# A DeltaNet block with a Fourier-mixing MLP on one core: the first sequence's opening is put in another order, and its first MLP products run ahead

## The chip, the cores and the metric

The kernel runs on 1 core of a Trainium2 chip. The core has TensorE (PE, matrix products into PSUM), VectorE (DVE), ScalarE (ACT), GpSimd (POOL) and SyncE (SP, whose queue issues most DMA transfers). Each of them works through its own instructions in a fixed order. The metric is the device time of one execution in microseconds.

## The reference

Inputs are q, k, v of shape (4, 8, 768, 48) in float32, beta of shape (4, 8, 768), and two weight matrices in float64. First a delta rule, for each of 4 sequences and 8 heads, with a 48 x 48 state:

```
k_n = k / (norm(k) + 1e-6)
for t in range(768):
    y[t]  = q[t] @ state
    v_old = k_n[t] @ state
    state = state + beta[t] * outer(k_n[t], v[t] - v_old)
```

The heads are laid side by side, which gives x of shape (4, 768, 384). Then:

```
mixed = real(fft(fft(x, axis=seq), axis=model))
u  = x + mixed
un = (u - mean(u)) / sqrt(var(u) + 1e-6)
out = u + max(un @ w_ch1, 0) @ w_ch2          # 384 -> 1536 -> 384
```

All is computed in float32 on the chip.

## The kernel before

**Delta rule.** A "load" g is 128 positions of one sequence, all 8 heads; a sequence has 6 loads (NL), 24 in all. A load is two chunks of 64 positions. Within a chunk the sequential rule becomes the inverse of a triangular matrix of 64 x 64. `pre_a` (L297) transposes the keys to KT on PE and forms their products G and GU. `invert16` (L432) inverts, for four loads at a time (a "round"), the 16 x 16 diagonal blocks by 15 pairs of DVE instructions (L491, L494), and then transposes the result on DVE to G and A (L497, L499). `pre_m16` (L572), for the loads 0 to 11, builds the whole inverse from these: Z and MT are masked copies on ACT (L582, L594), followed by four products on PE (Z with GU, MT with ND, Z with ND, MT with ND), with DVE steps at L605 and L609 and ACT steps at L591 and L607 between them; V is scaled at L613; for the loads 0 to 5 it then forms WT and U (L634, L635) in 32 small products of MT with K and V. `pre_q` (L505) makes QT and the masked product LQ (L529). `step(g, c)` (L641) is the recurrence, two dependent PE-DVE hops per chunk, and `outputs` (L705) gives x in two parts (L725 on ACT, L735 on DVE).

**Fourier part.** `folds` (L742) forms sums and differences of x along the sequence and the model axis, 8 DVE instructions for each of three t. `fourier` (L777) multiplies them with the tables evt and odt on PE (`sums`, into PSUM tiles pf), copies the result to F on ACT (L814), mirrors F (L819), and for each of six blocks T of 128 positions multiplies F with dtab and adds to x on DVE (L837 to L845), with mean and variance; POOL makes rstd (L848, L849).

**MLP.** `mlp` (L853): a group g is two blocks T. `scaled` makes un (L863), transposes it on PE (ptr) to unT (L868). Then 12 first products ph for fc = 0 to 11, each with Relu to hT (L880), and for each of the two blocks a second product po of 12 parts, added to x and stored (L890, L891). With its yields the MLP of one sequence has 75 pieces.

**Weights.** `weights` (L221) loads float64 as pairs of 32-bit words in twelve pieces of 768 KB, six of w1 (256 columns, i.e. two fc, each) and six of w2, two in flight, and converts each one: ACT L257, DVE L259, L261, L263, ACT L266, DVE L268, L269, POOL L272. A piece has five yields; `convert(n)` takes n of them for w1, w2's six follow in `conv`.

**Order.** Up to the end of the first products of sequence 0 the order of PE, DVE, ACT and POOL is written out by hand: generators are advanced one yield at a time (`advance`, `drain`, `fill` for inverse 1 and the folds). A loop over g = 0 to 5 does the recurrence of load g beside `pre_m16` of loads g+1 and g+2, the conversion of w1 and, from g = 4, the folds and keys of round 2. After it come the Fourier part and the first MLP products. From there on only PE's order is written out; the other engines' order is set by a scheduler. `period(g)` (L942) does the loads 6 to 23, six slots each, and advances the MLP of the sequence before (`side`) to a given number of pieces per slot (L1000); for sequence 0 thirteen pieces are done when it starts. `conv` and inverse 2 (for the loads 8 to 11) run under the first of these periods.

**Buffers.** A tag names a set of buffers that tiles share in turn: "big" has two (LQ6, the weights' ring, hT), "unT" two, "F" one, "M" one, "O" one; PSUM has the tags "pair", "one" and "post", two buffers each.

Of the kernel before, what the change touches and what calls it, by code (L numbers as in the profile page):

```python
# [20 lines left out]
RL = 4  # L21
# [43 lines left out]
def kernel(  # L65
# [15 lines left out]
    NC = NL  # L81
# [139 lines left out]
    def weights():  # L221
# [21 lines left out]
        for i, (_, dst) in enumerate(pieces):  # L243
            if i % half == 0:
                ring = wk.tile([128, 2, n, 2], I32, tag="big", bufs=2, name="w64")
                stage(i)
                stage(i + 1)
                yield
            lo, hi = ring[:, i % 2, :, 0], ring[:, i % 2, :, 1]
            if i < half:  # L250
                man = wk.tile([128, n], F32, tag="unT", bufs=2, name="man")
                num = wk.tile([128, n], I32, tag="unT", bufs=2, name="num")
            else:
                tmp = wk.tile([128, 2, n], F32, tag="O", name="wtmp")
                man, num = tmp[:, 0], tmp[:, 1].bitcast(I32)

            nc.scalar.activation(man, lo.bitcast(U32), ACT.Copy, scale=2.0 ** -52, bias=1.0)  # L257
            yield
            nc.vector.tensor_scalar(num, hi, 0xFFFFF, None, op0=ALU.bitwise_and)  # L259
            yield  # L260
            nc.vector.scalar_tensor_tensor(man, num, 2.0 ** -20, man, op0=ALU.mult, op1=ALU.add)  # L261

            nc.vector.tensor_scalar(num, hi, 20, 0x7FF, op0=ALU.logical_shift_right,  # L263
                                    op1=ALU.bitwise_and)
            yield
            nc.scalar.activation(num, num, ACT.Relu, bias=low_e)  # L266
            yield
            nc.vector.tensor_scalar(num, num, 255, 2.0 ** 23, op0=ALU.min, op1=ALU.mult)  # L268
            nc.vector.scalar_tensor_tensor(num, hi, -2 ** 31, num, op0=ALU.bitwise_and,  # L269
                                           op1=ALU.bitwise_or)  # L270
            c = dst.shape[1]
            nc.gpsimd.tensor_tensor(dst, man.rearrange("p (c f) -> p c f", c=c),  # L272
                                    num.bitcast(F32).rearrange("p (c f) -> p c f", c=c),
                                    op=ALU.mult)
            if i % half + 2 < half:
                stage(i + 2)
            yield
# [294 lines left out]
    def pre_m16(g):  # L572
# [20 lines left out]
        for e in range(2):  # L593
            nc.scalar.activation(MT[:, :, e, :], MTd[:, m8, :], ACT.Copy, scale=m_blk[:, e:e + 1])  # L594
        flat = "p m b t -> p (m b t)"
        yield
        for i in range(3):
# [14 lines left out]
        V = Vs.pop(g)  # L612
        (nc.vector if g < 2 * RL else nc.gpsimd).tensor_tensor(  # L613
            V.rearrange("p c j d -> p (c j) d"), V.rearrange("p c j d -> p (c j) d"),
            nT[:, m8, None].broadcast_to([128, 8, D]), op=ALU.mult)
# [161 lines left out]
    def fourier(b):  # L777
# [8 lines left out]
        def sums(a, par, tab, n, ts):  # L786
            if ts[0] == 0:
                pas[a, par] = ps_one()[:, 0:2 * n].rearrange("p (i k) -> p i k", i=2) if b else \
                    ps_post([128, 2, n], "pf")
# [9 lines left out]
        for a in range(2):  # L799
            for par, tab, n, hi in tabs:  # L800
                if b or a:
                    sums(a, par, tab, n, range(TH))
                elif par == 0:
                    for p2, t2, n2, _ in tabs:
                        sums(0, p2, t2, n2, range(TH - 1))
                    yield
                    for p2, t2, n2, _ in tabs:
                        sums(0, p2, t2, n2, (TH - 1,))
# [8 lines left out]
            for i in range(2 * a, 2 * a + 2):  # L817
                n = parts[i][2] - parts[i][1]
                nc.scalar.activation(F[0:n, i, HALF + 1:SEQ], F[0:n, i, HALF - 1:0:-1], ACT.Copy)  # L819

        norms = normed[b] = []
        for T in range(NC):
            tt = T % GT
            ks = slice(128 * T, 128 * T + 128)

# [27 lines left out]
    def mlp(b):  # L853
# [17 lines left out]
        unT = scaled(0)  # L871
        yield
        for g in range(NC // GT):
            hT = wk.tile([128, KF, GT * 128], F32, tag="big", bufs=2, name="hT")
            for fc in range(KF):
                ph = ps_post([128, GT * 128], "ph")
                for dt in range(KD):
                    mm(ph, w1[:, dt, 128 * fc:128 * fc + 128], unT[:, dt, :], dt == 0,
# [3 lines left out]
            for tt in range(GT):  # L882
                T = GT * g + tt
                po = ps_post([128, DM], "po")
                for fc in range(KF):
                    mm(po, hT[:, fc, 128 * tt:128 * tt + 128], w2[:, fc, :], fc == 0,
                       fc == KF - 1)
                    if fc % 2 == 1 and fc < KF - 1:
                        yield
                nc.vector.tensor_tensor(x[:, T, :], x[:, T, :], po, op=ALU.add)  # L890
                nc.sync.dma_start(out=out_v[b, T], in_=x[:, T, :])  # L891
                yield

                if tt == 0 and g + 1 < NC // GT:
                    unT = scaled(g + 1)
                    yield

# [44 lines left out]
    def period(g, side):  # L942
# [43 lines left out]
        for i in range(SLOTS):  # L986
# [13 lines left out]
            want = (PIECES - KEEP) * (SLOTS * n + i + 1) // (SLOTS * NL)  # L1000
# [8 lines left out]
    with tc.manual_schedule(engines=engines):  # L1009
# [48 lines left out]
        spin(1)  # L1058
        drain(qs[0])
        advance(ms[0])  # L1060
        advance(ms[1], 2)
# [3 lines left out]
        advance(qs[1])  # L1065
        drain(keys[-1])
        advance(ms[0])
        advance(ms[1])
        advance(inv1, 6)
        drain(ms[0])  # L1070
        advance(ms[1])
# [3 lines left out]
        fd = iter(())  # L1075
# [15 lines left out]
        for g in range(NL):  # L1091
# [4 lines left out]
            if g > 0:  # L1096
                advance(c0)
                fill(3)
            if g > 1:
                convert(1)  # L1100
            if g == 2:
                drain(inv1)
            if g > 0:
                advance(nm)
                advance(late)
            advance(n2)
            advance(c0)
            fill(3)
            if g == 0:
                advance(nm)  # L1110
            advance(n2)
            if g > 0:
                drain(late)
            if g == 4:
                fold = folds(0)
            if g >= 4:
                fd = part(fold, 8)
                advance(keys[g - 4])
            if g + 1 < NL:
                drain(qs[g + 1])  # L1120
            advance(nm)
            advance(c1)
            fill(3)
            if g > 0:
                convert(2)
            drain(nm)
            advance(n2)
            if g + 1 < NL:
                advance(c1)
            fill(3)  # L1130
            if g > 0:
                convert(2)
            advance(n2)
            if g + 2 < NL:
                advance(qs[g + 2])
            if g >= 4:
                drain(keys[g - 4])
# [5 lines left out]
            if g == 2:  # L1143
# [3 lines left out]
                load_q(NL + 1)  # L1147
        convert(1)
        drain(late)
        late = None  # L1150
        drain(ms[-1])
        load_beta(2)

        drain(fold)
        f = fourier(0)
        advance(f)
        for i in range(4):
            advance(f)
            convert((2, 1, 1, 1)[i])
        advance(keys[2])  # L1160
        advance(f)
        drain(keys[2])
        advance(f)
        advance(keys[3])
        side, done = mlp(0), 0
        advance(side)
        drain(keys[3])
        for T in range(2, NC):
            while converted < min(30, 5 * (T // 2 + T % 2)):
                convert(1)  # L1170
            advance(f)
            advance(side)
        for fc in range(NC - 2, KF):
            while converted < min(30, 5 * (fc // 2 + 1)):
                convert(1)
            advance(side)
        done = 1 + KF
# [48 lines left out]
```

## Time and profile before

| | us |
|---|---|
| median of 3 runs | 797.94 |
| the runs | 794.44, 797.94, 798.23 |
| profiled execution | 796.16 |
| its span | 794.4 |

| engine | busy us | share of the span |
|---|---|---|
| PE | 704.1 | 89% |
| PE weight loads | 544.2 | 69% |
| DVE | 372.5 | 47% |
| ACT | 243.9 | 31% |
| POOL | 99.2 | 12% |

Between span and time lie 1.8 us outside the first and last instruction. The 40 slices of the span (19.9 us each; digits are busy tenths, and tenths of full clock for PEclk) show where PE is not busy:

```profile
PE   5876676777599989999989999699999999999998
DVE  5857657569841496425189117984121141600000
ACT  3633354544333321323412333123223222221120
PEclk9999698879589999999989999899999999999999
```

Busy shares are averages over stages with different limits, so a stage is read by itself. A timeline row gives start, duration, engine, line, instruction, out<-in, shapes and count, and in brackets the idle time before it and what ended it. PE executes a float32 product as two records.

### The profile page before, as it was taken

The page shows a single profiled execution, that of the slowest core. Times are in us where ns is not written, and L with a number is a line of the kernel's source. Part 1 is how long each engine was busy: PE and PEld are TensorE (multiplying, and loading weights), DVE is VectorE, ACT ScalarE, POOL GpSimd, SP SyncE. Part 2 cuts the span into 40 slices and gives each one's busy share as a digit, 9 for nine tenths or more (in the row PEclk, how much of TensorE's full clock was granted, in tenths as well). Part 3 has the DMA queues.
Part 4 walks back from the last instruction along what each step waited for, and adds up shares of the span by engine and source line. Part 5 has one row for each costly group of instructions (what it writes and reads, how often), then busy time and mean ns, then how long its engine had stood idle before and what let it go on. Part 6 is the DMA issues. An engine that isn't in the chain of part 4 may idle for free. (4 is left out here: it accounts for less than half of the span.)

```text
span 794.4 us, 22940 instructions
## 1 busy us (share of the span) xinstructions
PE 704.1 (89%) x10164; PEld 544.2 (69%) x10164; DVE 372.5 (47%) x893; ACT 243.9 (31%) x588; POOL 99.2 (12%) x132
## 2 busy tenths in 40 slices
PE   5876676777599989999989999699999999999998
PEld 4665666766367857777857767577768677786784
DVE  5857657569841496425189117984121141600000
ACT  3633354544333321323412333123223222221120
POOL 7000010112220002201010102201100020100000
PEclk9999698879589999999989999899999999999999
DMA  9832143023412211101311121001120000000000
GB/s 149 213 56 60 38 118 78 11 91 104 111 28 50 55 27 44 24 11 37 56 32 42 33 42 42 11 11 26 31 51 18 22 12 1 18 3 20 11 10 21
DMA packets 109366, 36.08 MB, mean 45 GB/s; under 512 B 101682, under 2 KB 105043, under 8 KB 109267
## 3 DMA queue, kind: packets, MB, share of 16 engines
q1 hardware_dynamic: 107442, 33.86, 19.4%
q8 instruction: 80, 1.31, 0.7%
q0 software_dynamic: 640, 0.43, 0.4%
q10 hardware_dynamic: 1184, 0.33, 0.3%
q14 instruction: 20, 0.16, 0.1%
HBM read 29.88 MB, written 4.72 MB: 44 GB/s over the span
## 5 line engine op out<-in xcount | busy, mean ns | idle before, releaser
L110 PE MATMUL po<-w,hT 128*128 128x384 f32 x576 | 209.0, 504 | 0.9 <-ACT unT L868 0.9
L110 PE MATMUL ph<-unT,w 128*128 128x256 f32 x864 | 203.0, 386 | 1.8 <-ACT hT L880 1.3
L110 PEld LDWEIGHTS ph<-unT,w 128*128 128x128 f32 x864 | 160.2, 191 | 25.7 <-issue 1.6
L110 PEld LDWEIGHTS po<-w,hT 128*128 128x128 f32 x576 | 106.1, 194 | 59.9 <-issue 3.0
L880 ACT ACTIVATE hT<-ph 128x256 f32<-128x256 f32 x144 | 55.0, 383 | 157.1 <-PE ph L110 156.9
L890 DVE TENSOR_TENSOR x<-x,po 128x384 f32<-128x384 f32 x24 | 13.2, 551 | 123.1 <-PE po L110 123.1
L702 DVE TENSOR_TENSOR S<-S,pair 128x192 f32<-128x192 f32 x40 | 13.9, 348 | 91.0 <-PE pair L110 91.0
L110 PEld LDWEIGHTS one<-V,MT 64*64 64x64 f32 x768 | 31.6, 145 | 18.8 <-issue 12.3
L110 PE MATMUL one<-V,MT 64*64 64x48 f32 x768 | 37.0, 232 | 4.1 <-issue 2.9
L110 PE MATMUL one<-MT,ND 64*64 64x64 f32 x768 | 29.8, 231 | 7.8 <-ACT MT L607 7.1
L424 DVE TENSOR_TENSOR M<-M,tmp 128x31 f32<-128x31 f32 (+15 forms) x93 | 35.1, 377 | 2.8
L420 DVE TENSOR_TENSOR tmp<-A,M 128x31 f32<-128x31 f32 (+15 forms) x93 | 32.9, 354 | 2.8
L110 PEld LDWEIGHTS one<-MT,ND 64*64 64x64 f32 x768 | 27.4, 145 | 9.2 <-ACT MT L607 8.0
L543 POOL TENSOR_TENSOR MT<-A,pack 128x512 f32<-128x512 f32 x12 | 12.6, 1051 | 159.3 <-PE one L110 135.1
L661 DVE TENSOR_TENSOR V<-V,pair 128x192 f32<-128x192 f32 x33 | 11.6, 350 | 44.6 <-PE pair L110 42.1
L110 PE MATMUL one<-Z,GU 64*64 64x64 f32 x384 | 16.1, 243 | 18.3 <-ACT Z L582 18.3
L110 PEld LDWEIGHTS one<-dtab,F 97*128 97x128 f32 (+1 forms) x192 | 26.6, 202 | 5.2
L110 PEld LDWEIGHTS pair<-U,K 64*64 64x64 f32 x704 | 17.0, 143 | 17.0 <-issue 12.5
L110 PEld LDWEIGHTS one<-Z,GU 64*64 64x64 f32 x384 | 14.6, 156 | 19.6 <-ACT Z L582 19.6
L735 DVE TENSOR_TENSOR x<-x,pair 128x384 f32<-128x384 f32 x24 | 13.2, 552 | 29.8 <-ACT x L725 15.4
L110 PE MATMUL one<-dtab,F 97*128 97x97 f32 (+1 forms) x192 | 26.4, 283 | 0.0
L110 PE MATMUL pair<-KT 48*32 48x64 f32 (+1 forms) x1152 | 22.7, 247 | 4.0 <-ACT KT L295 3.9
(172 smaller groups left out, 997.7 us busy)
## 6 DMA issues: line engine op xcount, KB each, us to landing
w<-in_moe_w_ch_dram SPq DMA_DIRECT2D x12, 768.0 KB
out_dram<-x SPq DMA_DIRECT2D x24, 192.0 KB
K<-in_k_dram SPq DMA_DIRECT2D x92, 48.0 KB
V<-in_v_dram SPq DMA_DIRECT2D x92, 48.0 KB
C<-in_k_dram SPq DMA_DIRECT2D x18, 192.0 KB
Q<-in_q_dram SPq DMA_DIRECT2D x18, 192.0 KB
w<-in_q_dram SPq DMA_DIRECT2D x6, 192.0 KB
evt<-k_even SPq DMA_DIRECT2D x1, 579.0 KB
```

The source lines that it names most:

```text
L110: nc.tensor.matmul(o, lhsT=lhsT, rhs=rhs, start=start, stop=stop, skip_group_check=True)
L420: nc.vector.tensor_tensor(t, A[:, j + 1:W, j:j + 1].broadcast_to([128, n, j + 1]), M[:, j:j + 1, 0:j + 1].broadcast_to([128, n, j + 1]), o ...
L424: nc.vector.tensor_tensor(M[:, j + 1:W, 0:j + 1], M[:, j + 1:W, 0:j + 1], t, op=ALU.add)
L543: nc.gpsimd.tensor_tensor(MT, MTd[:, m8, None, :].broadcast_to([128, 8, 2, W]), m_blk[:, None, :, None].broadcast_to([128, 8, 2, W]), op=A ...
L661: nc.vector.tensor_tensor(R4, R4, pw[:, :, 0:2 * D].rearrange("p a (j e) -> p a j e", e=D), op=ALU.subtract)
L702: nc.vector.tensor_tensor(s1v, s0.rearrange("p h j e -> p h (j e)"), pk, op=ALU.add)
L735: nc.vector.tensor_tensor(xv, xv, pl[:, :, 0:4 * D], op=ALU.add)
L880: nc.scalar.activation(hT[:, fc, :], ph, ACT.Relu)
L890: nc.vector.tensor_tensor(x[:, T, :], x[:, T, :], po, op=ALU.add)
```

## The change

It concerns sequence 0 up to the end of its MLP; the arithmetic is the same.

- **Opening.** For load 0, MT's masks go to DVE and V is scaled right behind them; one of six idle products (`spin`) goes; inverse 1 starts earlier among the products of loads 0 and 1.
- **Loop.** It runs over g = 0 to 4, with four `fill` steps per slot where there were three, and other places for the yields; `convert` is called less, so that 4 of 6 pieces of w1 are converted in loop and tail.
- **Load 5** is written out by itself: recurrence, outputs and folds. Load 7's `pre_m16` and the keys of loads 9 to 11 are moved behind it, between the first MLP products.
- **Transforms.** All four sums of `fourier(0)` are issued together, two in "post" and two in "one" banks; F is mirrored at T = 2 and not between them.
- **MLP of sequence 0.** Both first-product groups 0 and 1 come before the second products of group 0. The ring of w2 takes the tag "F", which F leaves after the last T; `man` takes the tag "M" from piece 3 on.
- **Periods 6 to 11.** The 50 pieces after the first thirteen are spread over all 36 slots.

```diff
@@ weights
-                ring = wk.tile([128, 2, n, 2], I32, tag="big", bufs=2, name="w64")
+                ring = wk.tile([128, 2, n, 2], I32, tag="F" if i else "big", bufs=1 if i else 2,
+                               name="w64")
...
-            if i < half:
+            if i == half // 2:
+                man = wk.tile([128, n], F32, tag="M", name="man")
+            elif i == 0:
@@ pre_m16
-            nc.scalar.activation(MT[:, :, e, :], MTd[:, m8, :], ACT.Copy, scale=m_blk[:, e:e + 1])
+            if g == 0:
+                nc.vector.tensor_scalar(MT[:, :, e, :], MTd[:, m8, :], m_blk[:, e:e + 1], None,
+                                        op0=ALU.mult)
+            else:
+                nc.scalar.activation(MT[:, :, e, :], MTd[:, m8, :], ACT.Copy,
+                                     scale=m_blk[:, e:e + 1])
...
+        V = None if g else scaled_v()
@@ fourier
-                pas[a, par] = ps_one()[:, 0:2 * n].rearrange("p (i k) -> p i k", i=2) if b else \
-                    ps_post([128, 2, n], "pf")
+                pas[a, par] = ps_one()[:, 0:2 * n].rearrange("p (i k) -> p i k", i=2) \
+                    if b or a else ps_post([128, 2, n], "pf")
...
-                elif par == 0:
-                    for p2, t2, n2, _ in tabs:
-                        sums(0, p2, t2, n2, range(TH - 1))
+                elif (a, par) == (0, 0):
+                    for a2 in range(2):
+                        for p2, t2, n2, _ in tabs:
+                            sums(a2, p2, t2, n2, range(TH - 1))
                     yield
...
+            if T == TH - 1:
+                for i in range(4):
+                    n = parts[i][2] - parts[i][1]
+                    nc.scalar.activation(F[0:n, i, HALF + 1:SEQ], F[0:n, i, HALF - 1:0:-1],
+                                         ACT.Copy)
@@ mlp
+        if b == 0:
+            turns = [rows_of(0), first_of(0), rows_of(1), first_of(1), second_of(0, 0),
+                     second_of(0, 1), rows_of(2), second_of(1, 0), second_of(1, 1), first_of(2)]
+        else:
+            turns = [rows_of(0), first_of(0), second_of(0, 0), rows_of(1), second_of(0, 1),
+                     first_of(1), second_of(1, 0), rows_of(2), second_of(1, 1), first_of(2)]
@@ period
-            want = (PIECES - KEEP) * (SLOTS * n + i + 1) // (SLOTS * NL)
+            ready = 0 if b > 1 else 1 + KF
+            want = ready + (PIECES - KEEP - ready) * (SLOTS * n + i + 1) // (SLOTS * NL)
@@ the loop (now g = 0 to 4)
+                advance(c0)
+                fill(4)
+                if g > 1:
+                    convert(1)
+                if g == 2:
+                    drain(inv1)
+                    advance(n2)
                 advance(nm)
                 advance(late)
+                advance(c0)
+                fill(4)
+                advance(n2)
+                drain(late)
...
                 advance(nm)
+                advance(c1)
+                fill(3)
+                convert(2)
+                drain(nm)
+                advance(n2)
+                advance(c1)
+                fill(3)
+                convert(1)
@@ after the loop
+        g = NL - 1
+        c0, c1 = step(g, 0), step(g, 1)
...
+        late = outputs(g)
+        advance(late)
+        advance(fold, 8)
+        drain(late)
...
+        advance(ms[6])
         f = fourier(0)
         advance(f)
+        drain(fold)
+        advance(f, 4)
         advance(f)
+        advance(ms[7])
         advance(f)
         side, done = mlp(0), 0
         advance(side)
+        rest = [ms[7], ms[6], keys[1], ms[7], keys[1], ms[7], keys[2], ms[7], keys[2], ms[7], keys[3],
+                keys[3]]
+        for fc in range(KF):
             while converted < min(30, 5 * (fc // 2 + 1)):
                 convert(1)
             advance(side)
+            if fc % 2 == 0 and fc < 8:
+                advance(f)
+            drain(rest[fc]) if fc == 1 else advance(rest[fc])
```

## The prediction

> **What bounds the kernel now.** I read the 40 slices first, then the granted clock and busy time in stretches cut at landmarks of TensorE's (PE's) order, then the list of waits of PE, then the timeline of each engine. In the stretches the columns are the length, the busy time of PE, PE's weight loads, VectorE (DVE), ScalarE (ACT) and GpSimd (POOL), the granted clock, the DMA share and GB/s.
>
> ```profile
> 119.25:168.19 48.94, 34.19 (x641) 31.08 (x637) 30.38 (x64) 23.19 (x58) 6.81 (x8) 0.80 0.26 72
> 168.19:189.86 21.67, 20.41 (x98) 17.80 (x98) 18.81 (x53) 8.81 (x22) 3.79 (x5) 0.91 0.12 38
> 189.86:218.07 28.21, 14.47 (x289) 10.92 (x288) 25.12 (x56) 9.96 (x17) 7.37 (x5) 0.67 0.47 124
> 218.07:345.00 126.93, 120.79 (x2010) 91.57 (x2011) 63.09 (x143) 38.00 (x90) 17.61 (x17) 0.97 0.18 36
> 382.00:794.40 412.40, 393.42 (x4468) 291.51 (x4468) 144.57 (x363) 100.77 (x260) 37.91 (x45) 0.98 0.11 24
> ```
>
> From 218 us on PE is busy 95% or more at a clock near 1: work put there costs its length, and work taken from there is a gain. Before that PE idles, and its order waits for DVE and ACT. So the change is judged by when PE reaches one landmark, the product of group 8's Z with GU (218.07 us), and by how many MLP products it has done by then. The waits, seen by PE between 30 and 222 us (total, times, longest), and four places in the timeline (in brackets the idle time before, and who ended it):
>
> ```profile
> PE one L110 <- ACT Z L582: 18.3, 6, 7.6
> PE one L110 <- ACT MT L607: 7.1, 6, 2.5
> PE one L110 <- DVE Z L605: 5.2, 6, 1.6
> PE ptr L113 <- DVE un L863: 4.5, 1, 4.5
> ```
> ```profile
> 45.81 0.31 PE L110 MATMUL one<-V,MT 64*64 64x48 f32 x1 [2.70 <-issue]
> 84.12 1.86 PE L110 MATMUL one<-Z,GU 64*64 64x64 f32 x29 [6.65 <-ACT Z L582]
> 163.84 1.54 PE L113 MATMUL ptr<-pack,un 128*128 128x128 f32 x6 [4.49 <-DVE un L863]
> 218.07 1.97 PE L110 MATMUL one<-Z,GU 64*64 64x64 f32 x32 [7.61 <-ACT Z L582]
> ```
>
> **Profiled execution and median.** The sum is made against the profiled execution, 796.16 us; the median is 797.94, 1.8 us more, and I add that 1.8 at the end. A tenth of a microsecond is counted per handover between engines (DVE's subtraction ends at 107.49, PE starts at 107.64). Worked this way, one step of the loop before comes out at 13.0 us; measured is 13.07 (100.68 to 113.75).
>
> **1. The opening.** Before, V of load 0 is scaled at 45.15 us, behind 14 DVE instructions, and PE stands 2.70 us, then runs at half clock for 3 us. After, the scaling (0.56) and the two mask products of MT (0.33 each) follow the transposes, and are done at 36.0. But more is now ahead of load 1, which lands no earlier (its last V product 55.8 against 55.86); load 2's comes at 66.2 against 69.2.
>
> **2. Inverse 1.** It gets four DVE pairs per slot instead of three and three slots in step 0, so that in step 2 only its last three operations and two transposes (2.0 and 1.95) remain. The wait of 6.65 becomes two of 2.4 and 1.9. Load 3's last V product: 81.3 to 82.3, against 91.5.
>
> **3. Steps 3 and 4.** Z's two masks (0.45 each) go ahead of x on ACT, MT (0.6) ahead of the conversion's ACT step, and the LQ product ahead of the transpose. The waits of 0.98 and 1.18 us per step go; the next late thing is V (L613, 0.55 behind L735's 0.56). A step becomes 11.05 us instead of 13.07, 11.6 with a key transpose. Load 5's last V product: X = 104.0 to 107.5, I take 105.8 (half of the clock loss seen from 76 to 93) against 119.25: **-13.5**.
>
> **4. Outputs, folds, transforms.** Before, X to the first MLP product is 48.9 us (119.25 to 168.19). After: step 5 by the pair buffers ends at X+12.6; folds of t=1 (8 DVE instructions, 3.7) end at 15.5, of t=2 at 20.2; 32 records of pf from 15.65 to 22, partly at half clock, 16 more to 24.5; four banks are emptied by 25.2; then the first T product at 25.3, the two T on DVE (2.1 each) with POOL's 0.95 to 32, un 0.45, and 2.6 to the first MLP product as from 163.30 to 165.9: X+34.7. **-14.2**; it leaves out load 7's 4.4 us of PE and three key products of 1.3, which come next.
>
> **5. The first products.** Before 21.7 us. After, 8 of them with load 7, four T and keys end at t = X+58.6 (at half clock up to X+41.5, as from 164 to 172), so 23.9 us. Here is the price: w1's piece 4 (columns of product 8) and piece 5 (of 10) are converted only now. In DVE's order of the changed kernel piece 4 stands behind MT of load 7, whose product is just ahead of product 8 on PE, and it alternates with piece 6. Piece 6's load waits on SP until tile F is read (t-3.0) and lands 4.6 us later. From t: MT's add 0.79; AND 0.55; piece 6's AND, held by its load, 2.3; two L261 (0.95) 4.05; two L263 (0.56) 5.0; ACT L266 (0.94, from 4.6) 5.54; L268 0.56 and L269 0.96 to 7.16; POOL 1.81 to 9.06. PE waits **9.15**. Piece 5 stands behind pieces 6 and 7, which share one buffer and so wait for POOL each: piece 6's product is over at 12.85, piece 7's at 19.9, then piece 5's L261 21.4, L263 22.75, ACT 23.7, L268 and L269 25.4, POOL 27.26. PE, done with product 9 at 12.5, waits **14.85**. The last key product ends at t+32.85. Sum 56.75 against 21.67: **+35.1**.
>
> **6. From there to the landmark.** Before 28.2 us. After, ACT's queue holds the next QT until piece 8's product lets piece 9's, and that one's lets piece 10's, first step start (t+37.4): PE starts again at 38.9. Pieces 10 and 11 end at 45.75 and 55.25; inverse 2, which now begins only after the late keys, has 29 operations of 0.30 and five others behind that, then the transpose of 2.0 (t+66.6) and Z's two masks: 67.6. PE arrives at t+68.1 by its own work, too. 35.2 against 28.2: **+7.0**.
>
> **7. What has been done by then.** One transposed group (0.9) and 10 first products (13.0) more than before, less one pair of second products (1.46): **-12.4**, since PE is full afterwards. DVE and ACT steps of these (hT, un) lie beside PE. PE's half clock from 218 to 221.5 goes: **-1.8**. The wait of 3.1 us at 295 (ptr for L890) may go, as un of group 2 is ready early: 0 to -3.1, I take **-1.5**.
>
> Loads and queues: the V loads stand ahead of beta on SP now, need a free buffer, and landed early enough before. SP is held by piece 6's load only up to t-3. ScalarE's mirrored copies (4 of 0.47) lie behind product 0 and are needed by T=3 only. From the second image on the orders are as before.
>
> Sum: -13.5 - 14.2 + 35.1 + 7.0 - 12.4 - 1.8 - 1.5 = -1.3; 794.9 for the profiled run, 796.7 as a median. Ends: step 3 -15.3 to -11.7; step 5 +29 (piece 5 taken by the row of DVE work alone, 7 pieces of 3.6) to +39 (each piece 8.2, the mean of pieces 6 to 11 before, for 6.9); step 7 -14 to -6.
>
> **Two rules of the Trainium skill.** PE's clock is 0.50 from 46 to 48 us after 2.7 us of idling, and from 77 to 84 and beyond after 6.65. "TensorE: Matmul & The Clock Gate", section on HAM oscillation, says that the clock halves after idle gaps above some 3.4 us; here a shorter one did. The two long waits of part 5 would halve it by either; by the row the work between them is hidden by DVE's chain. L494 took 1.81 us, not 0.28, at 76.56, while POOL's 1.81 us product ran. "SBUF — State Buffer", section "Who interferes with whom", says that DVE and GpSimd lock a shared port pair for a whole instruction, also for DVE instructions with two SBUF inputs. By the row, an instruction next to a POOL product is 1.5 longer where DVE isn't waiting for POOL anyway (four of the eight products, counted above); if the rule hit at all eight, the sum would be +4.7.
>
> **Rivals.** (a) Slower: the filler is thin. The changed kernel spreads 50 pieces over the 36 slots of loads 6 to 11, so 39 are left after the landmark for 28 slots, 1.4 each, where 49 were, 1.75 each. If a slot with one product (1.3 us) doesn't cover the chain PE-DVE-PE-ACT, waits come back and the 12.4 is not kept. For it: before, slots without filler show waits of 0.7 to 2.7 us (191 to 203). Against it: slots with one product (274.80) show none. Half of it lost gives 803, all 809; it decides from 5 us on. (b) Faster: the clock. If step 2's two short waits and step 5's pauses (2 us at most) don't halve it, X is 104, the 32 pf records take 4.3 us and not 6.3, and products 0 to 2 come 4 us sooner: -8, so 789. For it: pauses of 1.2 us from 100 to 119 left it at 1.00. Against: 2.7 us did not. (c) The parts are done as described, since the compiled order shows them; that conversions block PE less than I count would need another order on DVE.
>
> **How the numbers follow.** 0.5% of 797.94 is 4 us, about what a measurement of this kernel can tell. My sum, near no change: 0.35; its own range 793 to 801. Faster (b): 0.33. Slower (a), or part 5 at its upper end: 0.32. The range 786 to 809 leaves out some 0.2 of both tails.
>
> **What would show it.** Right: PE's waits of 9 and 15 us before MLP products 8 and 10 of the first group, released by POOL L275; the loop steps at 11 us; the first pf at about 121 us; the landmark at 230 to 236; no wait on Z there. Wrong: if products 8 and 10 wait under 10 us together the kernel is 10 us faster than said; if waits above 6 us show between the landmark and 345, (a) holds.

## The result, and the profile after

The changed kernel takes 795.04 us (median of 20 runs, 793.73 to 799.01), the kernel before 795.19 (20 runs, 793.31 to 798.34). The ratio is 0.9995, with a 95% interval of 0.9981 to 1.0009: no change. The forecast was 796.7 and "near no change". The span of the profiled execution is 793.9 us, against 794.4.

PE's timeline of the changed kernel at the places that the prediction names (start, duration, instruction, out<-in, and in brackets the idle time before it and what ended it):

```profile
136.91 1.54 PE L113 MATMUL ptr<-pack,un 128*128 128x128 f32 x6 [5.01 <-DVE un L881]
139.12 2.90 PE L110 MATMUL ph<-unT,w 128*128 128x256 f32 x6 [0.67 <-ACT unT L886]
171.38 2.93 PE L110 MATMUL ph<-unT,w 128*128 128x256 f32 x6 [9.46 <-POOL w L275]
189.58 2.93 PE L110 MATMUL ph<-unT,w 128*128 128x256 f32 x6 [11.60 <-POOL w L275]
200.83 0.69 PE L110 MATMUL pair<-QT,KT 48*64 48x64 f32 x32 [4.26 <-ACT QT L298]
228.21 1.15 PE L110 MATMUL one<-Z,GU 64*64 64x64 f32 x32 [0.23 <-ACT Z L585]
```

The first MLP product starts at 139 us instead of 168. Then PE waits 9.5 and 11.6 us for POOL's product L275, the last step of converting a piece of w1. The product of group 8's Z with GU, the landmark of the prediction, comes at 228.2 instead of 218.1, without a wait.

The stretches between these landmarks (length; busy time of PE, PE's weight loads, DVE, ACT, POOL with counts; granted clock; DMA share; GB/s):

```profile
105.83:139.12 33.29, 22.76 (x427) 20.68 (x424) 21.46 (x50) 9.98 (x26) 2.75 (x3) 0.81 0.21 48
139.12:195.98 56.86, 35.80 (x341) 29.40 (x342) 32.92 (x59) 24.98 (x51) 13.12 (x13) 0.72 0.27 81
195.98:228.21 32.23, 26.21 (x352) 20.71 (x351) 29.91 (x69) 14.14 (x32) 6.31 (x4) 0.89 0.25 57
228.21:345.00 116.79, 107.36 (x1943) 79.25 (x1944) 57.73 (x138) 31.47 (x76) 14.24 (x15) 0.97 0.19 40
382.00:793.90 411.90, 392.44 (x4472) 290.79 (x4470) 144.67 (x363) 100.98 (x260) 37.89 (x45) 0.99 0.11 24
```

The first line was 48.9 us before, the second 21.7, the third 28.2. The landmark is 10.1 us later, and the rest, 793.9 - 228.2 = 565.7 us, is 10.6 shorter than 794.4 - 218.1 = 576.3: what was won by running ahead is about what was lost before the landmark. PE's waits between 228 and 345 us (total, times, longest):

```profile
PE one L110 <- DVE E L781: 3.9, 1, 3.9
PE pair L110 <- DVE S L716: 2.9, 3, 2.6
PE one L110 <- DVE V L675: 1.7, 1, 1.7
```

### The profile page after: what moved, and what is told of

It is laid out like the page before. It is cut to its first block, busy times and chain, and to the rows that moved or that the text cites. A ratio compares the mean times of both kernels' runs of the same rounds, so it can differ in the third digit from the quotient of the medians.

```text
span 793.9 us, 22923 instructions
## 1 busy us (share of the span) xinstructions
PE 701.6 (88%) x10162; PEld 539.7 (68%) x10162; DVE 376.3 (47%) x895; ACT 244.5 (31%) x586; POOL 99.1 (12%) x132
## 5 line engine op out<-in xcount | busy, mean ns | idle before, releaser
L110 PE MATMUL ph<-unT,w 128*128 128x256 f32 x864 | 213.6, 398 | 22.8 <-POOL w L275 21.1
L110 PE MATMUL po<-w,hT 128*128 128x384 f32 x576 | 206.0, 498 | 0.6 <-ACT unT L886 0.6
L110 PEld LDWEIGHTS ph<-unT,w 128*128 128x128 f32 x864 | 164.2, 197 | 49.2 <-POOL w L275 21.7
L716 DVE TENSOR_TENSOR S<-S,pair 128x192 f32<-128x192 f32 x40 | 13.8, 346 | 91.1 <-PE pair L110 91.1
L110 PE MATMUL one<-V,MT 64*64 64x48 f32 x768 | 35.4, 226 | 4.0 <-DVE V L675 2.3
L423 DVE TENSOR_TENSOR tmp<-A,M 128x31 f32<-128x31 f32 (+15 forms) x93 | 34.9, 375 | 2.8
L855 DVE TENSOR_TENSOR x<-x,one 128x193 f32<-128x193 f32 x24 | 8.4, 350 | 52.0 <-ACT Q L851 51.5
L675 DVE TENSOR_TENSOR V<-V,pair 128x192 f32<-128x192 f32 x33 | 11.6, 352 | 43.5 <-PE pair L110 34.4
L110 PEld LDWEIGHTS pair<-U,K 64*64 64x64 f32 x704 | 15.9, 137 | 17.4 <-issue 14.5
L110 PEld LDWEIGHTS pair<-KT 48*32 48x32 f32 (+1 forms) x1152 | 18.7, 136 | 8.3 <-ACT KT L298 4.7
L110 PE MATMUL pair<-U,K 64*64 64x48 f32 x704 | 21.3, 229 | 2.8 <-issue 1.7
```

What stands on the lines that cost most here:

```text
L110: nc.tensor.matmul(o, lhsT=lhsT, rhs=rhs, start=start, stop=stop, skip_group_check=True)
L423: nc.vector.tensor_tensor(t, A[:, j + 1:W, j:j + 1].broadcast_to([128, n, j + 1]), M[:, j:j + 1, 0:j + 1].broadcast_to([128, n, j + 1]), o ...
L675: nc.vector.tensor_tensor(R4, R4, pw[:, :, 0:2 * D].rearrange("p a (j e) -> p a j e", e=D), op=ALU.subtract)
L716: nc.vector.tensor_tensor(s1v, s0.rearrange("p h j e -> p h (j e)"), pk, op=ALU.add)
L855: nc.vector.tensor_tensor(near, near, pb[:, 0, 0:MH + 1], op=ALU.add)
```

## The experiments

The question is not whether time was saved. By landmarks the opening and the loop save 13.4 us (load 5's last V product at 105.83 instead of 119.25), the part from there to the first MLP product 15.7, with work postponed, and the work ahead 10.6. The question is what takes it back. The theory was PE's two waits for pieces 4 and 5 of w1; the rivals were the thin filler behind the landmark and VectorE's queue. All times are medians. Each ratio, with its 95% interval behind it, is to runs of the kernel before on the same chip (medians of 793.8 to 795.0 us).

### Pieces 4 and 5 early, and PE's wait taken away alone

```
 (first products 0 to 11 of the changed kernel)
-            while converted < min(30, 5 * (fc // 2 + 1)):
-                convert(1)
             advance(side)
+            convert((2, 2, 1, 2, 2, 1, 0, 0, 0, 0, 0, 0)[fc])
```

> The changed kernel, with pieces 4 and 5 of w1 converted beside the first MLP products 0 to 5 and not behind product 7; nothing else is edited. Theory (the two waits of 9.5 and 11.6 us before products 8 and 10 lie on the path, and are the price of the change): both waits go; the last key product ends at about 170 us instead of 196.0; inverse 2's first transpose on DVE starts at about 173 instead of 197.4, and the product of group 8's Z with GU, 31.7 us behind it, at about 205 instead of 228.2; time 775 (770 to 781). Rival (DVE's conversions of w2 and inverse 2 set that product anyway, or waits come back behind it): the product stays above 220, or PE's waits between it and 345 us grow by over 10 us; time 788 to 796.

Measured: 786.53, ratio 0.9884 (0.9849 to 0.9919). Both waits are gone, and the last key product of round 2 starts at 169 us instead of 195. But only 8.5 us of the 20 that the theory gave come through: PE now waits 14.5 us at the landmark, which comes at 214.5 and not at 205. The time lies between the two ranges.

```
-                    mm(ph, w1[:, dt, 128 * fc:128 * fc + 128], un[g][:, dt, :], ...
+                    wc = fc - 8 if b == 0 and g == 0 and fc >= 8 else fc
+                    mm(ph, w1[:, dt, 128 * wc:128 * wc + 128], un[g][:, dt, :], ...
```

> The changed kernel, with the first products 8 to 11 of group 0 reading the columns of products 0 to 3 of w1, so that PE doesn't wait for pieces 4 and 5; these are still converted where the change has them. (Left out: these four products are not those of the reference.) Theory (waits on the path, and DVE's chain behind them the next limit): both waits go, the last key product ends at about 170, but 7.2 us of conversions more than with an early conversion stand ahead of inverse 2: Z with GU at 210 to 215, time 779 to 784. Rival 1 (only PE's waits count): as with early conversion, 775. Rival 2 (DVE sets everything): Z with GU above 222, time 790 to 796.

Measured: 793.66, ratio 0.9974 (0.9954 to 0.9993). This kernel leaves out four first products of the reference: others stand in their place. With 21 us of PE's waits gone, 1.3 us are won. The last key product starts at 178.1 us, 8 later than the theory has it, since PE waits 2.2 and 6.1 us for copies of ACT ahead of it. The two rows of PE's landmark, first with pieces 4 and 5 early, then with PE's wait alone taken away:

```profile
214.47 1.98 PE L110 MATMUL one<-Z,GU 64*64 64x64 f32 x32 [14.49 <-ACT Z L585]
```
```profile
222.35 1.97 PE L110 MATMUL one<-Z,GU 64*64 64x64 f32 x32 [12.31 <-ACT Z L585]
```

And the stretch from load 7's last product to that landmark in the same two kernels:

```profile
163.38:214.47 51.09, 32.80 (x441) 25.77 (x439) 46.55 (x92) 24.48 (x51) 13.66 (x11) 0.83 0.36 104
```
```profile
162.00:222.35 60.35, 34.81 (x443) 27.46 (x441) 55.20 (x101) 26.81 (x54) 17.91 (x13) 0.82 0.35 94
```

DVE (third busy time) works 91% of both stretches. It has the conversions of six and eight pieces to do there, and inverse 2 among them. PE no longer waits for w1; it waits at Z instead. So rival 2 of the second run holds: behind 162 us DVE's queue sets the landmark, and PE's waits for w1 were mostly cover for it. An early piece pays because its DVE work moves to where DVE idles: from 126 to 162 us the changed kernel keeps DVE busy for 14.2 of 36.0 us, the one with early pieces for 21.6.

### The pace of before

```
-            ready = 0 if b > 1 else 1 + KF
+            ready = 0
```

> The changed kernel with the pace of before for the MLP of sequence 0: nothing in the first seven slots of the periods, then 1.75 pieces per slot. Theory (work done ahead of the product of group 8's Z with GU is kept): about 10 first products fall behind that product, which waits for Z at about 227 all the same; 8 to 12 us slower, 803 to 807. Rival (a) of the prediction (the thin filler gives the work back as waits): PE's waits from that product to 345 us fall from 9 to under 5 us, and the time is 788 to 796.

Measured: 800.97, ratio 1.0074 (1.005 to 1.0097). The landmark is at 229.3, now with a wait for Z:

```profile
229.26 1.97 PE L110 MATMUL one<-Z,GU 64*64 64x64 f32 x32 [8.46 <-ACT Z L585]
```

Behind it PE waits 2.1 us up to the start of the second sequence's transforms, where the changed kernel waits 5.4, and another 1.9 there instead of 3.9:

```profile
PE ptr L113 <- DVE x L913: 1.2, 1, 1.2
PE pair L110 <- DVE S L716: 0.9, 1, 0.9
```

The waits fall as the rival said, and the time still rises, though by less than the theory said: 800.97 lies between the two ranges. So the thin filler has a price, but the even pace is worth 5.9 us net. It doesn't take the gain back.

### The opening and the loop alone

The kernel before, with the changed opening, inverse 1 and loop for loads 0 to 4. Load 5 (in the old form, in the new loop's variables), the Fourier part, the weights, the MLP and its pace are those of before.

> The kernel before with the changed opening and the changed loop for loads 0 to 4 alone; load 5, the Fourier part, the weights, the MLP and its pace are those of before. Theory (a rigid shift): load 5's last V product at 106 to 108 instead of 119.25, everything behind it as much earlier, Z with GU at 205 to 208; time 782 to 786. Rival (conversions and inverse 2, which keep DVE busy 25.1 of 28.2 us ahead of Z with GU, or the landing of the weights, set that product): it stays above 214; time 790 to 796.

Measured: 780.32, ratio 0.9808 (0.9783 to 0.9834). The landmark is at 202.2 instead of 218.1, with the same wait on Z (7.6 us) and with the same rest behind it (778.7 - 202.2 = 576.5 us). It is nearly a rigid shift, 14.7 us in the time, 1.7 us more than the theory's range allows:

```profile
202.21 1.98 PE L110 MATMUL one<-Z,GU 64*64 64x64 f32 x32 [7.59 <-ACT Z L582]
```

This part alone is better than the whole change.

### The loop and the work ahead

```
 (weights)
-                ring = wk.tile([128, 2, n, 2], I32, tag="big", bufs=2, name="w64")
+                ring = wk.tile([128, 2, n, 2], I32, tag="F" if i else "big", bufs=1 if i else 2, ...
 (mlp: the turns of the changed kernel; period:)
-            want = (PIECES - KEEP) * (SLOTS * n + i + 1) // (SLOTS * NL)
+            ready = 0 if b > 1 else 1 + KF
+            want = ready + (PIECES - KEEP - ready) * (SLOTS * n + i + 1) // (SLOTS * NL)
```

> The kernel before with the changed opening and loop (as in the run of these alone, 780.3 us) and with the changed order of the MLP of sequence 0: both first-product groups ahead of second products, w2's ring in the tag F, the 50 pieces spread over 36 slots. Load 5, the Fourier part, the keys of round 2 and the conversions of w1 are those of before. Theory (the two halves of the gain, the loop's 15 us and the work ahead of 10.6, are independent, and what costs them in the changed kernel is the order of load 5, the keys and w1's pieces): Z with GU at 202 to 206 with 10 first products more done, time 767 to 773. Rival (running ahead needs DVE's time, so that the product with GU goes later by what is done ahead): Z with GU above 210, time 777 to 783.

Measured: 773.61, ratio 0.9714 (0.9656 to 0.9773). The landmark is at 204.5, with no wait, and 568.4 us are left behind it:

```profile
204.46 1.11 PE L110 MATMUL one<-Z,GU 64*64 64x64 f32 x32
```

The theory holds for the landmark, and the time is 0.6 us above its range: running ahead costs the landmark 2 us and shortens the rest by 8. A second measurement of the same kernel, further down, gave 775.97. What remains of the change (load 5, load 7, the keys and w1's pieces in their new places, and the four banks) is thus worth 19 to 21 us to the wrong side.

### Inverse 2 into the idle time

From the changed kernel: pieces 4 and 5 are converted from the last transform on, in the buffer O, so that M and unT are free; the keys of loads 9 to 11 go beside products 0 to 2, and the steps of loads 6 and 7 and the transforms T shift with them; inverse 2 is advanced by hand.

```
-            if i == half // 2:
-                man = wk.tile([128, n], F32, tag="M", name="man")
...
-            elif i >= half:
+            elif i >= 4:
                 tmp = wk.tile([128, 2, n], F32, tag="O", name="wtmp")
...
+            if fc > 2:
+                advance(inv, 4)
```

> The changed kernel with pieces 4 and 5 of w1 converted from the last transform on, in the buffer O that w2's pieces use later (so that M and unT are free), the keys of loads 9 to 11 beside the first products 0 to 2, and inverse 2 advanced by hand beside the products 3 to 11. Theory (the product of group 8's Z with GU is set by DVE's order between 126 and 212 us, where DVE idles 19 us and then works without a pause): with inverse 2 in that idle time PE reaches Z with GU by its own work at 196 to 202 and doesn't wait there; PE's waits from 162 us to it are under 8 us; time 765 to 772. Rival (w2's pieces, now beside inverse 2, are late for the second products): waits of second products for POOL's products of w2 above 8 us behind it, time 775 to 785.

Measured: 784.58, ratio 0.987 (0.9819 to 0.9921). The time lies in the rival's range, but neither mechanism came: no wait of PE for POOL's products of w2 shows behind the landmark, and though Z is ready in time, PE reaches the landmark only at 216.4, with 11.8 us of waits from 162 us on. One of the holds, in ACT's row and PE's behind it:

```profile
170.04 0.26 ACT L456 ACTIVATE nrm<-A 128x32 f32<-128x32 f32 x1 [7.26 <-DVE A L450]
170.71 2.90 PE L110 MATMUL ph<-unT,w 128*128 128x256 f32 x6 [3.01 <-ACT hT L900]
```

Written out by hand, inverse 2's square root stands in ACT's queue ahead of the Relu of two products, waits there 7.3 us for DVE's transpose, and PE waits 3.0 us for a Relu behind it.

The same kernel with inverse 2 left to the scheduler again (the `advance(inv, 4)` goes):

> As the run with inverse 2 advanced by hand (784.6 us), but inverse 2 is left to the scheduler again, as in the changed kernel; pieces 4 and 5 of w1 are early and in O, the keys of loads 9 to 11 stand beside products 0 to 2. Theory (late keys hold inverse 2; the hand-written order added its own holds, such as ScalarE's 7.3 us at the square root): inverse 2's first transpose at 155 to 162 instead of 174.0 (run with early pieces alone) and 197.4 (changed kernel), Z with GU without a wait at 200 to 207, time 770 to 778. Rival (the holds come from conversions and transforms of one queue and not from inverse 2): PE idles as long as with the order by hand, Z with GU above 212, time 782 to 787.

Measured: 779.51, ratio 0.9805 (0.9773 to 0.9836). Inverse 2's first transpose starts at 154.4 us, and the landmark comes without a wait, as the theory has it, but at 210.3, 3 us later than its range; the time is 1.5 above it. Here the first transpose waits 2.0 us for the last copy of the keys' G, and in the changed kernel it starts 1.4 us behind the last key product: late keys had held inverse 2. The order by hand had cost 5 us by the medians; the two intervals just overlap, but every run of this kernel is faster than every run of the other. Against the kernel with the loop and the work ahead 5.9 us are left, 3.5 by its second measurement. From load 5's last V product to the landmark, here and then there, the latter in its first and in its second measurement:

```profile
104.60:210.25 105.65, 86.73 (x1113) 72.07 (x1111) 78.56 (x170) 46.37 (x108) 18.59 (x18) 0.81 0.28 75
```
```profile
106.20:204.46 98.26, 78.20 (x1117) 67.25 (x1114) 75.30 (x172) 46.26 (x108) 20.04 (x19) 0.90 0.30 82
105.30:206.25 100.95, 81.35 (x1118) 69.93 (x1114) 75.88 (x173) 46.51 (x108) 19.39 (x19) 0.83 0.29 79
```

PE has as many records in all three, 1113 to 1118, but needs 86.7 us for them at a mean clock of 0.81, where the other kernel needs 78.2 at 0.90 and 81.4 at 0.83. The lengths differ by 7.4 and 4.7 us, PE's busy time by 8.5 and 5.4. So in this account what is left is time that PE works at half clock, not time that it waits. That the landmark would come earlier by as much at full clock was not tried in this kernel.

### A key moved, and the four banks

Both start from the kernel with the loop and the work ahead.

```
-        advance(keys[1])
...
             convert((2, 1, 1, 1)[i])
+            if i < 2:
+                advance(keys[1])
+        drain(keys[1])
```

> The kernel with the changed loop and the work ahead (773.6 us), with the keys of load 9 moved from load 5's recurrence to the transforms, where PE waits for ScalarE and VectorE. Theory: PE's wait of 3.97 us for the GU copies of these keys goes, and load 5's outputs, folds and transforms come up to 4 us earlier: 769.5 to 772. Rival (the keys' six copies on ScalarE now stand ahead of F's or Q's copies, or inverse 2 comes later by as much): 773 to 777.

Measured: 774.91, ratio 0.9744 (0.9714 to 0.9774). The wait of 4.0 us is gone and the last folds are met 3 us earlier (131.8 instead of 134.9), but the first transposes of un start only 0.7 earlier (147.9), and the landmark stays (204.2): the rival.

The four banks are a swap of the function `fourier` for that of the changed kernel. For this run and the next the starting kernel was measured again beside them.

> The kernel with the changed opening, loop and MLP order again, to be compared with the two that follow on the same chip: 771 to 775 us.

Measured: 775.97, ratio 0.9761 (0.9731 to 0.9792).

> The kernel with the changed loop and the work ahead, with the four sums of the transforms issued together into four banks and F mirrored at T = 2, as the change has it. Theory (PE's wait there was only 0.3 us, for the last folds, so nothing was held by two banks): within 1.5 us of the kernel it is made from. Rival (the second half's sums, now ahead of ScalarE's first copies, bring T and un earlier by the 2 us that ScalarE's copies of F and the mirrored ones take): 2 to 4 us faster.

Measured: 774.85, ratio 0.9747 (0.9722 to 0.9772), 1.1 us under its starting kernel, with intervals that overlap: nothing that shows, as the theory has it.

### Idle products in three waits

An idle product is one whose result nothing reads.

```
+        def keep(n):
+            held = ps_post([128, 512], "held")
+            for _ in range(n):
+                nc.tensor.matmul(held[:, 0:DM], lhsT=ident, rhs=evt[:, 0, 0:DM], start=True, ...
...
+        advance(late)
+        keep(4)
         drain(late)
...
         side, done = mlp(0), 0
+        keep(5)
...
-                    drain(pre_q(NL))
+                    nq = pre_q(NL)
+                    advance(nq)
+                    keep(3)
+                    drain(nq)
```

> The kernel with the changed loop and the work ahead, with 12 idle products of 128x384 (some 0.8 us each at full clock, from the row of the idle products of the opening) in three waits of PE: 4 behind the first product of load 5's outputs, 5 ahead of the first transposes of un, 3 behind the transposes of load 6's queries. Theory (PE's clock is set in fixed steps of 3.41 us, and halves after a step in which PE was busy less than about half): the waits of 4.0, 4.5 and 3.3 us halve it for 6.8, 10.2 and 3.4 us; with the idle products the clock stays at 1.00 from 120 to 185 us, and of the 10 us lost at half clock the 3 to 6 that PE's own work bounds come back: 768 to 771, 3 to 6 less than the kernel it is made from. Rival (the idle products push later work as much as the clock gains, or the clock falls all the same): within 2 us of it, or slower.

Measured: 771.25, ratio 0.9697 (0.9673 to 0.9721), 4.7 us under the kernel that it is made from, measured beside it. The interval lies under that one's (0.9731 to 0.9792), though not under that of its first measurement, whose median is 2.4 us above this. What was the largest of the three waits (4.5 us, ahead of the first transposes of un), in PE's timeline:

```profile
144.37 3.39 PE L1084 MATMUL held<-evt,pack 128*128 128x384 f32 x10
149.03 1.00 PE L113 MATMUL ptr<-pack,un 128*128 128x128 f32 x6 [1.26 <-DVE un L875]
```

The stretch from 120 to 150 us, with the idle products and then without them:

```profile
120.00:150.00 30.00, 23.51 (x322) 19.03 (x318) 20.84 (x45) 13.66 (x36) 4.87 (x6) 1.00 0.15 34
```
```profile
120.00:150.00 30.00, 19.74 (x267) 18.22 (x268) 19.90 (x43) 12.39 (x33) 4.86 (x6) 0.77 0.08 16
```

The idle products do nothing but hold the clock at 1.00 (last column but two), and the landmark comes at 202.2 instead of 206.3. From load 5's last V product to it:

```profile
107.80:202.24 94.44, 79.10 (x1142) 64.83 (x1139) 76.78 (x173) 46.22 (x108) 19.29 (x19) 0.98 0.32 85
```

That is 94.4 us against the 98.3 and 101.0 of the two measurements without idle products. The clock still fell once, from 179 to 182.5 us, where no idle product stands.

### A rising pace

```
-            want = ready + (PIECES - KEEP - ready) * (SLOTS * n + i + 1) // (SLOTS * NL)
+            at, all_ = SLOTS * n + i + 1, SLOTS * NL
+            want = ready + (PIECES - KEEP - ready) * at * (3 * all_ + at) // (4 * all_ * all_)
```

(for sequence 0's MLP; the others keep theirs)

> The kernel with the changed loop, the work ahead and the idle products (771.3 us), with the 50 pieces of the MLP of sequence 0 at a rising pace (three quarters of the even share at the start, five quarters at the end) and not evenly. Theory (rival (a) of the prediction in the small: behind the product of group 8's Z with GU the even share leaves the last slots thin, and PE waits 1.7, 1.6 and 3.6 us at 280, 289 and 312 us, 6.9 together): the three waits fall under 4 us, and the time to 768 to 770. Rival (the filler taken from the first slots is missed there, or the last wait is for the folds and not for want of filler): 771 to 775.

Measured: 769.12, ratio 0.9679 (0.965 to 0.9708). PE's waits behind the landmark, with the even pace first and with the rising one second:

```profile
PE one L110 <- DVE E L779: 3.6, 1, 3.6
PE pair L110 <- DVE S L714: 2.1, 4, 1.6
PE one L110 <- DVE V L673: 1.7, 1, 1.7
PE one L110 <- ACT ND L592: 1.5, 1, 1.5
```
```profile
PE pair L110 <- DVE S L714: 2.3, 1, 2.3
PE one L110 <- DVE E L779: 1.9, 1, 1.9
PE ptr L113 <- DVE x L907: 1.9, 1, 1.9
PE one L110 <- DVE V L673: 0.2, 1, 0.2
```

The three named waits fall from 6.9 to 4.4 us, not under 4 as the theory has it, and a new one of 1.9 comes at 255. The median is 2.1 us lower, but the intervals overlap and the two profiled spans (767.9 and 768.1) are equal: whether the pace helps stays open. This kernel has the lowest median of all, 3.2% under the kernel before; the one without the rising pace has 3.0%.

## Why the prediction was right, and where it was not

The total was right: -1.3 us said, -0.5 in the profiled spans. That it came so near is in part luck: steps 4 and 6 were 4.4 us too long and step 7 was 5.1 us too good, and these cancel. By its steps (X is load 5's last V product):

| step | said | measured |
|---|---|---|
| 1, 2: load 1's, 2's, 3's last V product | 55.8, 66.2, 81.3 to 82.3 | 56.9, 67.2, 82.8 |
| 2: two waits for inverse 1's step | 2.4, 1.9 | 2.6, 1.6 |
| 3: one loop step; X | 11.05, 11.6 with a key; 105.8 | 11.3, 11.8; 105.8 |
| 4: X to the first MLP product | 34.7 | 33.3 |
| 5: waits; to the last key product | 9.15, 14.85; 56.75 | 9.46, 11.60; 56.9 |
| 6: to the landmark | 35.2 | 32.2 |
| 7: the landmark to the end, against before | -15.7 | -10.6 |

**Steps 1 to 5** follow the instruction order of the changed kernel with the durations of the trace before, and hold within 1.5 us each, but for the second wait: it is 3.3 shorter because PE comes to it later. The product after the first wait ran at half clock (2.93 us for six records, where 1.46 is usual). The sum of the step is as said. Step 5 also said that four of eight POOL products would cost DVE 1.5 us each. So it was: DVE's instructions at 169.58, 187.90, 205.85 and 213.88 us took 2.16, 2.44, 1.67 and 1.48 us where their like take 0.56, 0.96, 0.20 and 0.19, each beside a product of POOL. The Trainium skill's "SBUF — State Buffer", "Who interferes with whom", has both engines lock a shared port pair. The trace agrees in these times, and the four others fall where DVE was waiting anyway or in its transpose of 1.93 us, which isn't lengthened.

**Step 6** was 3.0 us too long: 1.2 because load 7's end to the last key product took 34.1 us and not 32.85, and 1.8 because inverse 2's chain let PE go at t + 66.3 and not 68.1. PE started again at t + 38.9, to the tenth as said. (t is the end of load 7's last product, 161.9 us.) With step 4's 1.4 us the landmark, 228.2, lies just below the 230 to 236 that were given.

**Step 7** was 5.1 us too good. The half clock and the wait of 3.1 at 295 us went, as said; but PE's waits from the landmark to 345 are 9.3 us, where before has 6.0 and the step counted 1.5 less than that: 4.8 of the 5.1. With the pace of before they fall to 4.0, so the thin filler sets more than half of them. This is rival (a), at two fifths of the 12.4 that it put at stake. By its own mark, waits above 6 us, it holds; it stayed just under the 5 us from which it was to decide, and steps 4 and 6 erred the other way. The sum took zero for it; the error of step 7 is that zero.

**The condition that fell.** The prediction said that the kernel would be 10 us faster if products 8 and 10 waited under 10 us together. With the waits alone removed the landmark moved by 5.9 us of the 21, and the time by 1.3 (3.9 in the profiled spans). As a sum along PE's order steps 5 and 6 are right; as a statement of cause step 5's "here is the price" is wrong. Most of the 21 us lay beside work that DVE had to do before the landmark in any case. Step 6 would have shown it, had it been worked for DVE alone: of the 66.3 us from load 7's end to the landmark 53.2 are DVE's work.

**Rival (b)**, a faster kernel by a clock that isn't halved, didn't come: the clock halved at 116, 133, 164, 181, 201 and 215 us. That it is worth some microseconds is shown by the idle products, 2.4 to 4.7 in another kernel.

**What the change is made of.** The opening and the loop: -14.7 us. The MLP's order and pace on top: -6.7, or -4.4 by the second measurement. Four banks: nothing that shows. Load 5, load 7, the keys and w1's last two pieces in their new places: +20, from 774.9 to 795.0. Of this, early pieces take back 8.5, and with them early keys and the other buffers 15.5; PE's half clock covers the remaining 5 us in the account of busy times above. But the clock falls by the pauses that an order makes, and load 5's own order was not tried by itself, so what causes these 5 us is open.

## What to carry to other kernels

A long wait of one engine is not a price until the queue that it waits for has been added up: take the busy time of the other engine between two landmarks, and where it is most of the length (80 and 91% here), move its work to where it idles before touching the wait. Try the parts of a large change one at a time, since a sum of zero can hide a part worth 2%. And look at the granted clock in PE's waits of 2 to 5 us: a few idle products can be cheaper than the half clock that follows, as 12 of them were here.

## What the runs showed of the hardware

PE's clock moves in fixed steps. The times at which it changed, read in slices of 0.2 us from 100 to 215 us, lie at multiples of some 3.4 us from each other in every kernel: with pieces in O and early keys at 108.3, 121.9, 135.5, 149.3, 159.5, 166.3, 183.3 and 190.1, which are distances of 13.6, 13.6, 13.8, 10.2, 6.8, 17.0 and 6.8 us. Cut in these steps, the first change of that kernel reads:

```profile
104.84:108.25 3.41, 1.71 (x58) 1.48 (x56) 3.17 (x8) 0.85 (x2) 0.00 (x0) 1.00 0.42 59
108.25:111.66 3.41, 3.41 (x103) 3.14 (x99) 1.80 (x3) 1.95 (x4) 0.00 (x0) 0.50 0.38 70
111.66:115.08 3.42, 2.55 (x82) 2.31 (x80) 2.40 (x5) 1.98 (x6) 1.37 (x1) 0.50 0.28 43
115.08:118.49 3.41, 2.05 (x76) 2.05 (x80) 2.56 (x6) 0.45 (x1) 0.43 (x1) 0.50 0.75 242
118.49:121.90 3.41, 3.41 (x52) 3.15 (x46) 3.25 (x8) 0.04 (x1) 0.00 (x0) 0.50 0.02 5
121.90:125.32 3.42, 3.42 (x22) 3.40 (x21) 3.28 (x8) 0.00 (x0) 0.00 (x0) 1.00 0.00 0
```

In the first step PE is busy for half the time, though no pause is longer than 1.0 us. The next four run at half clock, though the first of them has no pause, and the clock is back after the fourth, which has none either. In six kernels, the one before among them, some 205 such steps between 40 and 225 us ran at full clock. All with PE busy 0.50 or less were followed by half clock, none with 0.65 or more, and between these it went both ways: 26 of the 29 falls came after 0.51 or less, the others after 0.55, 0.63 and 0.64. The clock came back only after steps with some 0.90 or more, 31 times, and seven times not even then. These edges are not sharp: later on, in the kernel before, a step with 0.45 kept the clock (from 335.95 us), and with early pieces one with 0.82 brought it back (from 401.44 us). The steps stand where they happen to: the same kernel, profiled twice, ran 10.2 us at half clock at one pause and 3.4 at the same pause of the other execution (from 177 us on); a pause of 2.1 us at 120 us halved the clock in the first, one of 2.0 at 119 us did not in the other. Its mean clock from load 5 to the landmark was 0.83 and 0.90. So a pause of some 2 us halves the clock or not by where it falls. The Trainium skill's "TensorE: Matmul & The Clock Gate", Part 1, says that the window is 3413 ns and free-running, which agrees; the rule of its section on HAM oscillation, weighed in the prediction (gaps above some 3.4 us), is the case in which the place doesn't matter, since so long a pause leaves one step half empty wherever it falls. Here steps that were half busy were enough.
